# A third of the early v loads moved from GpSimd's casting DMA queue to SyncE's queue, with the cast done by GpSimd

## The chip, the cores and the metric

The kernel runs on one core of a Trainium2 chip. The metric is the device time of one execution in microseconds (us); lower is better. The engines are named as in the profile: PE (TensorE, with PEld for its weight loads), ACT (ScalarE), DVE (VectorE), POOL (GpSimd) and SP (SyncE). "q0" is the DMA queue that POOL issues into, "q1" the one of SP.

## The reference

Attention with a relative position bias for 8 batches of 8 heads, 576 positions and head size 64, followed by a feed-forward layer on the 4608 tokens:

```python
scores = scale * np.matmul(q, k.transpose(0, 1, 3, 2))      # q, k, v: (8, 8, 576, 64) float32
scores = scores + bias.transpose(2, 0, 1)[None, :, :, :]    # by bucketed distance, per head
attn = softmax(scores)
x = np.matmul(attn, v)            # to (4608, 512)
h = x @ w_in                      # (512, 2048)
g = np.maximum(0.01 * h, h)
out = g @ w_out                   # (2048, 512) -> (4608, 512) float32
```

## The kernel before

Work goes by pairs of heads: `items` lists the 32 pairs (b, p), four to a batch, and n counts them. For pair n, `qk_mm` makes score tiles on PE, `exp` turns them into bf16 on ACT, `band` multiplies the part near the diagonal by the bias factors `hk` on DVE, `av_tails` and `av` multiply by v on PE one pair later, and DVE divides by the row sums (`rcp`, `opair`). `x_transposes` turns the result into `xT`. When a batch is finished its tokens are ready for the feed-forward part, in token tiles T of 512: `ffn_in` (line 420) and `leaky` fill a buffer `gt` (pool `gt`, two buffers of 16 KB a partition), and `ffn_out` (line 447) reads it. The pieces of the feed-forward part are put between the attention steps from pair 4 on (`moe`), and what is left runs at the end (`moe_rest`). All orders are written out by hand: each engine runs its instructions in the order in which the program issues them.

v is kept in bf16 in two buffers `vn[b % 2]`, laid out [128 positions, 4 chunks c of positions, 8 heads, 65], where column 65 holds ones; the last 64 positions are in `v4`. DRAM holds float32, so every load of q, k, v and the weights goes through POOL's DMA queue, which casts on the way. The calls that matter, in POOL's order before the change:

- ahead of the loop: q and k of batch 0 and single heads 0 to 3 of v (`load_v_head`, line 125), `load_qk(1, 0, 4)`, then heads 4 to 7 of batch 0's v in four pieces (`load_v_part`, line 119), then `load_qk(1, 4, 8)` (line 112);
- at n = 0 (`loads`, called by `begin`): the first half of `w_in` (line 235), batch 1's v in four pieces, its tail (line 132), the second half of `w_in`, the first half of `w_out` (line 239);
- at n = 2: q and k of batch 2's lower heads, the second half of `w_out`;
- from n = 5 on, for batch b + 1 while batch b runs: at p = 1, 2 and 3 a one-element copy `tick` (line 621) waits until pair n - 2 is done, and then the loads of the next batch are issued, those of v at p = 1 and p = 2.

SP's queue holds at the start the small loads of the bias factors (`load_hk`, `load_hk4`, lines 192 and 199, the last of them `load_hk(4, H)`), and later the DMA transposes of q, k (line 265) and of the attention's result (line 387) and the stores of the output (line 466).

Of the kernel before, what the change touches and what calls it, by code (L numbers as in the profile page):

```python
# [10 lines left out]
FP32 = mybir.dt.float32  # L11
BF16 = mybir.dt.bfloat16
# [25 lines left out]
def kernel(  # L38
# [10 lines left out]
    nc = tc.nc  # L49

    B, H, S, D = q.shape
# [4 lines left out]
    P = 128  # L56
    n_pairs = H // 2
    NJ = S // P
# [3 lines left out]
    TT = 512  # L62
    n_tt = NT // TT
    n_fc = DF // P
# [11 lines left out]
    gt_pool = ctx.enter_context(tc.tile_pool(name="gt", bufs=2))  # L76
# [17 lines left out]
    NBUF = 2  # L94
# [4 lines left out]
    vn = [per.tile([P, NJ, H, D + 1], BF16, name=f"vn{i}") for i in range(NBUF)]  # L99
# [9 lines left out]
    def load_qk(b, h0, h1):  # L109
        i = b % NBUF  # L110
        for src, dst in ((q, qn[i]), (k, kn[i])):
            nc.gpsimd.dma_start(  # L112
                out=dst[0:RQ, h0:h1, :, :].rearrange("r h c d -> r h (c d)"),
                in_=src[b, h0:h1, :, :].rearrange("h (r c) d -> r h (c d)", c=NC),
            )

    def load_v_part(b, chunks, h0=0, h1=H):
        for c in chunks:
            nc.gpsimd.dma_start(  # L119
                out=vn[b % NBUF][:, c, h0:h1, 0:D],  # L120
                in_=v[b, h0:h1, c * P : (c + 1) * P, :].rearrange("h s d -> s h d"),
            )

    def load_v_head(b, h):
# [2 lines left out]
            in_=v[b, h, 0 : NJ * P, :].rearrange("(c s) d -> s c d", s=P),  # L127
        )

    def load_v_tail(b):  # L130
        for e in range(2):
            nc.gpsimd.dma_start(
                out=v4[b % NBUF][e * SL : (e + 1) * SL, :, 0:D],
                in_=v[b, e::2, NJ * P : S, :].rearrange("h s d -> s h d"),
            )

    def clear_v(eng, i):
        eng.memset(v4[i][:, :, D : D + 1], 1.0)
        eng.memset(vn[i][:, :, :, D : D + 1], 1.0)
# [39 lines left out]
    for j, (u, lo, w, m) in enumerate(groups):  # L179
        copy = nc.scalar.copy if j % 3 == 2 else nc.vector.tensor_copy  # L180
        copy(out=ub[:, C0 + lo : C0 + lo + m * w].rearrange("h (m w) -> h m w", w=w),
             in_=e8[:, u : u + m].unsqueeze(2).to_broadcast([H, m, w]))
    row = ub[:, :]
    nc.vector.tensor_copy(
        out=ub[:, C0 - BAND + 1 : C0],
        in_=bass.AP(tensor=row.tensor, offset=row.offset + C0 + BAND - 1,
                    ap=[list(row.ap[0]), [-1, BAND - 1]]),
# [3 lines left out]
    def load_hk(h0, h1):  # L191
        nc.sync.dma_start(
            out=hk[:, h0:h1, :],
            in_=bass.AP(tensor=udr, offset=h0 * UW, ap=[[1, P], [UW, h1 - h0], [1, BW]]),
        )

    def load_hk4(p0, p1):
        for e in range(2):
            nc.sync.dma_start(
                out=hk4[e * SL : (e + 1) * SL, p0:p1, :],  # L200
                in_=bass.AP(tensor=udr, offset=(2 * p0 + e) * UW + SL + P,
                            ap=[[1, SL], [2 * UW, p1 - p0], [1, P + SL]]),
            )
# [3 lines left out]
    load_hk(2, 4)  # L207
    load_hk4(1, n_pairs)
    load_hk(4, H)

    def mirrored(t, lo, hi):

        w = t.shape[-1]
        v = t[..., w - hi : w - lo]
        ap = [list(d) for d in v.ap]
        ap[-1][0] = -1
        return bass.AP(tensor=v.tensor, offset=v.offset + hi - lo - 1, ap=ap)
# [4 lines left out]
    load_v_head(0, 0)  # L222
    load_v_head(0, 1)
    load_v_tail(0)
    load_qk(0, 6, H)
    load_v_head(0, 2)
    load_v_head(0, 3)
    load_qk(1, 0, H // 2)
    load_v_part(0, range(NJ), 4, H)
    clear_v(nc.gpsimd, 1)  # L230
    load_qk(1, H // 2, H)

    def load_w_in(half):
        o = slice(half * (DF // 2), (half + 1) * (DF // 2))
        nc.gpsimd.dma_start(out=w_in_sb[:, :, o], in_=moe_w_in[:, o].rearrange("(c p) f -> p c f", p=P))

    def load_w_out(half):
        n = n_fc // 2
        nc.gpsimd.dma_start(
            out=w_out_sb[:, half * n : (half + 1) * n, :],  # L240
            in_=moe_w_out[half * n * P : (half + 1) * n * P, :].rearrange("(f p) e -> p f e", p=P),
        )
# [3 lines left out]
    qts, kts, ops_ = {}, {}, {}  # L246
# [151 lines left out]
    gts = {}  # L398
    rest = {"on": False, "turn": 0}

    def bank(name):

        if rest["on"]:
            turn = rest["turn"] = (rest["turn"] + 1) % 6
            if turn % 3 == 0:
                return ps_o_pool.tile([P, 512], FP32, name=name, tag=f"o{turn // 3}")
            if turn % 3 == 1:
                return ps_s_pool.tile([P, 512], FP32, name=name, tag="ps_s")
        return ps_m_pool.tile([P, 512], FP32, name=name, tag="m")

    def ffn_in(T, f, spare=None):
        if f == 0:
            gts[T] = gt_pool.tile([P, n_fc, TT], BF16, name="gt")
        t0 = T * TT
        if spare is None:
            pm = bank("pm1")
        else:
            pm = ps_o_pool.tile([P, 512], FP32, name="pm1", tag=f"o{spare}")
        for c in range(n_cc):
            nc.tensor.matmul(pm, lhsT=w_in_sb[:, c, f * P : (f + 1) * P], rhs=xT[c][:, t0 : t0 + TT],  # L420
                             start=(c == 0), stop=(c == n_cc - 1))
        return pm
# [61 lines left out]
    def step(kind):  # L484
        T, s = made[kind], at_piece[kind]
        at_piece[kind] = (s + 1) % n_fc
        if at_piece[kind] == 0:
            made[kind] += 1
        return T, s
# [5 lines left out]
    def piece_in(spare=None):  # L495
        T, s = step("in")
        leaky(T, s, ffn_in(T, s, spare))
# [51 lines left out]
    def moe_block():  # L549

        done = 0
        while not can("out") and can("in") and done < 4 and room["left"] > 0:
            T, f = step("in")
            leaky(T, f, ffn_in(T, f, 0 if done == 3 and room["left"] > 1 else None), done == 1)
            room["left"] -= 1
            done += 1
            if done < 3:
                yield
        while done < 2:
            done += 1  # L560
            yield
        if room["split"]:
            yield
            piece_out()
            piece_out()
        elif can("out") and room["left"] >= 4:
            for part in range(4):
                piece_out()
                room["left"] -= 1
                if part == 1:  # L570
                    yield
            moe(2, 0 if room["left"] > 1 else None)
        else:
            yield
            moe(2)
        yield
# [28 lines left out]
    tick = per.tile([1, 1], BF16, name="tick")  # L605

    def loads(n):

        b, p = items[n]
        if n == 0:  # L610
            load_w_in(0)
            load_v_part(1, range(NJ))
            load_v_tail(1)
            load_w_in(1)
            load_w_out(0)
        elif n == 2:
            load_qk(2, 0, H // 2)
            load_w_out(1)
        if b < 1 or p < 1 or b > B - 2:
            return  # L620
        nc.gpsimd.tensor_copy(out=tick, in_=ops_[n - 2][0:1, 0, 0:1])  # L621
        if p == 1:
            load_qk(b + 1, H // 2, H)
            load_v_part(b + 1, (0,))
        elif p == 2:
            load_v_part(b + 1, (1, 2, 3))
        else:
            load_v_tail(b + 1)
            if b + 2 < B:
                load_qk(b + 2, 0, H // 2)  # L630

    def begin(n):
        loads(n)
        if by_dma(n + 1):
            turn_ahead(n)
# [53 lines left out]
    n = n_pairs  # L689
# [24 lines left out]
    for n in range(n_pairs + 1, N + 1):  # L714
# [41 lines left out]
        if room["only"]:  # L756
            exp(n, 3, ps_b)
            moe(2)
            exp(n, 4, ps_c)
            score(n, 5)  # L760
            T, f = step("in")
            room["left"] -= 1

            def last_bands():
                band(n, 5)
                band(n, 4)

            leaky(T, f, ffn_in(T, f), True, last_bands)
            moe(room["left"])
            continue  # L770
# [44 lines left out]
```

## Time and profile before

| | us |
|---|---|
| median of 3 runs (lowest, highest) | 378.06 (377.69, 379.08) |
| profiled execution, its own time | 378.04 |
| span in the profile | 376.3 |
| PE busy | 366.1 (97%) |
| ACT busy | 239.9 (64%) |
| DVE busy | 199.1 (53%) |
| POOL busy | 77.3 (21%) |

The span is the time from the first to the last instruction; what the profiled execution took beyond it, 1.7 us, lies around it. TensorE's granted clock is 1.0 throughout. Times in the profile are counted from the start of the span. A row of a timeline gives start, duration, engine, line, operation, output and input tile, the count, and in brackets the idle time ahead of it with what ended it. A row of a DMA issue gives output and input, the queue, the count, the size and the time from issue to landing.

### The profile page before, as it was taken

What the parts mean: (1) busy time and instruction counts of PE and PEld (TensorE: products, weight loads), DVE (VectorE), ACT (ScalarE), POOL (GpSimd) and SP (SyncE); (2) the same over time, 40 slices, a digit from 0 to 9 for tenths busy, and PEclk for the clock granted to TensorE, in tenths of its full rate; (3) what the DMA queues carried; (4) which work ended last, traced back from release to release, by engine and by line L of the source; (5) the groups of instructions that cost most, each with busy time, mean ns of one, the idle gap of its engine ahead of it and who ended that gap; (6) DMA issues with size and microseconds to landing.
All of it is one profiled execution on the core that took longest, in us unless ns stands there. A gap on an engine that the chain in (4) does not pass through costs nothing.

```text
span 376.3 us, 8737 instructions
## 1 busy us (share of the span) xinstructions
PE 366.1 (97%) x3604; PEld 186.7 (50%) x3604; DVE 199.1 (53%) x502; ACT 239.9 (64%) x376; POOL 77.3 (21%) x118
## 2 busy tenths in 40 slices
PE   7879999999999999999999999999999999999996
PEld 3455555554555555555545545555555544444442
DVE  3678577777657666666755666655553300200221
ACT  5998886568856787777866666767777255055000
POOL 8763422333023303330323033100000000000000
PEclk9999999999999999999999999999999999999999
DMA  8999999998599959997998399453111000110212
GB/s 104 189 194 186 206 199 120 181 179 121 77 119 157 145 85 123 151 152 91 142 118 132 72 124 127 74 79 77 47 47 47 28 30 0 59 54 0 82 60 84
DMA packets 104351, 40.06 MB, mean 106 GB/s; under 512 B 83184, under 2 KB 98808, under 8 KB 104312
## 3 DMA queue, kind: packets, MB, share of 16 engines
q0 software_dynamic: 53696, 18.36, 47.2%
q1 hardware_dynamic: 50472, 21.02, 31.7%
q8 instruction: 28, 0.46, 0.5%
q10 hardware_dynamic: 144, 0.13, 0.1%
q14 instruction: 11, 0.09, 0.1%
HBM read 37.68 MB, written 9.45 MB: 125 GB/s over the span
## 4 chain that ended last, share of the span: by engine, by line
PE 89%; DMA 5%; POOL 2%; DVE 2%; ACT 1%; issue 1%; DVEq 0%; ACTq 0%; POOLq 0%
PE pm L447 34%; PE pm L420 32%; PE ps_o L372 10%; PE ps_s L312 8%; DMA vn<-in_v_dram 3%; PE ps_s L315 2%; DMA v<-in_v_dram 1%; PE ps_o L361 1%; PE ps_q L305 1%; DVE opair L376 1%; PE ps_tx L394 1%; PE ps_t L275 1%; ACT at L325 1%; POOL kn L112 1%; POOL qn L112 0%
## 5 line engine op out<-in xcount | busy, mean ns | idle before, releaser
L420 PE MATMUL pm<-xT,w_in_sb 128*128 128x512 bf16 x576 | 138.4, 379 | 0.1
L433 ACT ACTIVATE gt<-pm 128x512 bf16<-128x512 f32 x138 | 82.5, 603 | 86.2 <-PE pm L420 85.7
L447 PE MATMUL pm<-w_out_sb,gt 128*128 128x512 bf16 x576 | 132.5, 379 | 0.0
L325 ACT ACTIVATE at<-ps_s 128x1024 bf16<-128x1024 f32 x128 | 124.2, 1028 | 8.2 <-PE ps_s L312 8.1
L348 DVE TENSOR_TENSOR at<-at,hk 128x768 bf16<-128x768 bf16 (+3 forms) x160 | 71.0, 453 | 32.7 <-ACT at L328 19.9
L447 PEld LDWEIGHTS <-gt 128*128 128x128 bf16 x576 | 53.0, 98 | 60.6
L420 PEld LDWEIGHTS <-w_in_sb 128*128 128x128 bf16 x576 | 52.0, 98 | 54.8 <-issue 0.7
L465 DVE COPY y<-pm 128x512 f32<-128x512 f32 x33 | 22.8, 691 | 76.6 <-PE pm L447 76.6
L372 PE MATMUL ps_o<-vn,at 128*128 128x65 bf16 x1280 | 49.8, 194 | 0.4 <-DMA vn<-in_v_dram 0.4
L372 PEld LDWEIGHTS <-at 128*128 128x128 bf16 x1280 | 44.7, 97 | 9.5 <-issue 1.2
L312 PE MATMUL ps_s<-qt,kt 64*128 64x512 bf16 x256 | 40.1, 381 | 3.5 <-ACT at L325 3.0
L375 DVE RECIPROCAL rcp<-ps_o 128x5 f32<-128x5 f32 x64 | 12.3, 192 | 45.1 <-PE ps_o L372 45.1
L376 DVE TENSOR_TENSOR opair<-ps_o,rcp 128x320 bf16<-128x320 f32 x64 | 31.5, 492 | 3.3
L119 POOL DMA_DIRECT2D vn<-in_v_dram x32 | 29.6, 931 | 10.0 <-PE ps_s L312 5.6
L621 POOL COPY tick<-opair 1x1 bf16<-1x1 bf16 x18 | 4.7, 263 | 130.8 <-DVE opair L376 130.8
L312 PEld LDWEIGHTS <-kt 64*128 64x128 bf16 x256 | 8.4, 94 | 29.0 <-issue 21.5
L332 ACT ACTIVATE at<-ps_s 128x576 bf16<-128x576 f32 x32 | 21.8, 681 | 0.2 <-PE ps_s L316 0.2
L328 ACT ACTIVATE at<-ps_q 128x256 bf16<-128x256 f32 x64 | 21.5, 402 | 0.3 <-PE ps_q L305 0.2
L457 ACT COPY y<-pm 128x256 f32<-128x256 f32 x1 | 0.4, 372 | 27.5 <-DVE y L457 27.5
L294 DVE COPY kt<-tu 128x576 bf16<-128x576 bf16 x23 | 15.5, 674 | 0.0
L290 DVE COPY qt<-tu 128x576 bf16<-128x576 bf16 x23 | 15.0, 650 | 0.4 <-DMA tu<-pr 0.4
L112 POOL DMA_DIRECT2D qn<-in_q_dram x18 | 14.1, 782 | 4.2 <-PE ps_t L275 1.3
(57 smaller groups left out, 175.0 us busy)
## 6 DMA issues: line engine op xcount, KB each, us to landing
out_dram<-y SPq DMA_DIRECT2D x35, 256.0 KB, 2.3
qn<-in_q_dram POOLq DMA_DIRECT2D x14, 288.0 KB, 5.9
kn<-in_k_dram POOLq DMA_DIRECT2D x14, 288.0 KB, 7.1
vn<-in_v_dram POOLq DMA_DIRECT2D x28, 128.0 KB, 5.2
w_in_sb<-in_moe_w_in_dram POOLq DMA_DIRECT2D x2, 1024.0 KB, 12.9
w_out_sb<-in_moe_w_out_dram POOLq DMA_DIRECT2D x2, 1024.0 KB, 15.9
qn<-in_q_dram POOLq DMA_DIRECT2D x4, 144.0 KB, 4.3
kn<-in_k_dram POOLq DMA_DIRECT2D x4, 144.0 KB, 4.6
```

The costliest lines, as they stand in the source:

```text
L119: nc.gpsimd.dma_start(out=vn[b % NBUF][:, c, h0:h1, 0:D], in_=v[b, h0:h1, c * P : (c + 1) * P, :].rearrange("h s d -> s h d"),)
L312: nc.tensor.matmul(ps[:, e, :], lhsT=kt[r, u * P : (u + 1) * P], rhs=qt[r, 0:512], start=True, stop=True)
L325: nc.scalar.activation(at[:, :, u, 0:512], ps, AF.Exp, scale=scale)
L328: nc.scalar.activation(at[:, e, :, 512:S], ps[e][:, 0 : NJ * SL].rearrange("p (c i) -> p c i", i=SL), AF.Exp, scale=scale)
L332: nc.scalar.activation(at4[:, 0:S], ps.rearrange("p e i -> p (e i)")[:, 0:S], AF.Exp, scale=scale)
L348: nc.vector.tensor_tensor(out=o, in0=o, in1=m, op=ALU.mult)
L372: nc.tensor.matmul(ps[:, ic, :], lhsT=at[:, o : o + P], rhs=vn[b % NBUF][:, c, 2 * p + e, :], start=False, stop=(ic == NJ and c == NJ - 1))
L376: nc.vector.tensor_tensor(out=opair[:, :, e * D : (e + 1) * D], in0=ps[:, :, 0:D], in1=rcp.to_broadcast([P, NJ + 1, D]), op=ALU.mult)
L420: nc.tensor.matmul(pm, lhsT=w_in_sb[:, c, f * P : (f + 1) * P], rhs=xT[c][:, t0 : t0 + TT], start=(c == 0), stop=(c == n_cc - 1))
L433: nc.scalar.activation(g, pm, AF.Prelu, bias=0.0, scale=1.0, alpha=0.01)
L447: nc.tensor.matmul(pm, lhsT=gt[:, f, ts * P : (ts + 1) * P], rhs=w_out_sb[:, f, :], start=(f == 0), stop=(f == n_fc - 1))
L465: nc.vector.tensor_copy(out=y, in_=pm)
```

## The change

The four pieces of batch 0's upper heads, batch 1's v and batch 2's v are no longer loaded by POOL's casting queue. SP's queue copies them as float32 into a buffer `stage` that takes one of the two buffers of pool `gt` (tag "gt"), and POOL casts them from there into `vn` with `tensor_copy`, one instruction for each chunk.

- Batch 0's upper heads: `stage_v` stands behind `load_hk(4, H)` in SP's order; `cast_v` stands behind `load_qk(1, 4, 8)` in POOL's, ahead of the first half of `w_in`.
- Batch 1: at n = 3 a one-element copy on DVE into `stage`, reading pair 1's result, stands ahead of the four transfers; the casts follow in POOL's order, and behind them the first half of `w_out`, the lower q and k of batch 2 and the second half of `w_out`, which stood at n = 0 and n = 2.
- Batch 2: the one-element copies on POOL at n = 5 and n = 6 write into `stage` and stand ahead of two transfers each; the casts come at n = 7. Batches 3 to 7 are loaded as before.

```diff
+    stage = gt_pool.tile([P, 2 * NJ, H, D], FP32, name="stage", tag="gt")
+
+    def stage_v(b, chunks, h0=0, h1=H):
+        for c in chunks:
+            nc.sync.dma_start(
+                out=stage[:, c, h0:h1, :],
+                in_=v[b, h0:h1, c * P : (c + 1) * P, :].rearrange("h s d -> s h d"),
+            )
+
+    def cast_v(b, h0=0, h1=H):
+        for c in range(NJ):
+            nc.gpsimd.tensor_copy(out=vn[b % NBUF][:, c, h0:h1, 0:D], in_=stage[:, c, h0:h1, :])
...
     load_hk(4, H)
+    stage_v(0, range(NJ), 4, H)
...
     load_qk(1, 0, H // 2)
-    load_v_part(0, range(NJ), 4, H)
     clear_v(nc.gpsimd, 1)
     load_qk(1, H // 2, H)
+    cast_v(0, 4, H)
...
-            gts[T] = gt_pool.tile([P, n_fc, TT], BF16, name="gt")
+            gts[T] = gt_pool.tile([P, n_fc, TT], BF16, name="gt", tag="gt")
...
         if n == 0:
             load_w_in(0)
-            load_v_part(1, range(NJ))
             load_v_tail(1)
             load_w_in(1)
+        elif n == 3:
+            nc.vector.tensor_copy(out=stage[0:1, 0, 0, 0:1], in_=ops_[n - 2][0:1, 0, 0:1])
+            stage_v(1, range(NJ))
+            cast_v(1)
             load_w_out(0)
-        elif n == 2:
             load_qk(2, 0, H // 2)
             load_w_out(1)
         if b < 1 or p < 1 or b > B - 2:
             return
-        nc.gpsimd.tensor_copy(out=tick, in_=ops_[n - 2][0:1, 0, 0:1])
+        done = ops_[n - 2][0:1, 0, 0:1]
+        if b == 1 and p < 3:
+            nc.gpsimd.tensor_copy(out=stage[0:1, 2 * p - 2, 0, 0:1], in_=done)
+            stage_v(b + 1, (2 * p - 2, 2 * p - 1))
+        else:
+            nc.gpsimd.tensor_copy(out=tick, in_=done)
         if p == 1:
             load_qk(b + 1, H // 2, H)
+        if p == 1 and b > 1:
             load_v_part(b + 1, (0,))
-        elif p == 2:
+        elif p == 2 and b > 1:
             load_v_part(b + 1, (1, 2, 3))
-        else:
+        elif p == 3:
+            if b == 1:
+                cast_v(b + 1)
             load_v_tail(b + 1)
```

## The prediction

> **What bounds the kernel now.** I read the page's head and its chain first, then busy time by stage, then the timelines of the stage in which PE has gaps.
>
> ```profile
> span 376.3 us, 8737 instructions
> ...
> PE 89%; DMA 5%; POOL 2%; DVE 2%; ACT 1%; issue 1%; DVEq 0%; ACTq 0%; POOLq 0%
> PE pm L447 34%; PE pm L420 32%; PE ps_o L372 10%; PE ps_s L312 8%; DMA vn<-in_v_dram 3%; PE ps_s L315 2%; DMA v<-in_v_dram 1%; PE ps_o L361 1%; PE ps_q L305 1%; DVE opair L376 1%; PE ps_tx L394 1%; PE ps_t L275 1%; ACT at L325 1%; POOL kn L112 1%; POOL qn L112 0%
> ```
>
> The chain is PE's for 89%; the transfers on it are those of `v`, 4% together. Busy time by stage (length, then PE, PEld, DVE, ACT, POOL) shows where PE is not full:
>
> ```profile
> 17.00:23.00 6.00, 4.72 (x104) 3.22 (x99) 5.06 (x15) 5.52 (x8) 2.10 (x3) 1.00 1.58 199
> 23.00:29.00 6.00, 4.74 (x98) 3.18 (x97) 4.40 (x13) 5.52 (x8) 4.76 (x6) 1.00 1.28 201
> 29.00:35.00 6.00, 5.66 (x98) 3.53 (x95) 4.84 (x13) 5.72 (x10) 1.58 (x2) 1.00 1.99 176
> ...
> 120.00:298.00 178.00, 178.00 (x1843) 91.47 (x1842) 108.22 (x270) 127.28 (x201) 28.88 (x42) 1.00 0.75 99
> ```
>
> From 120 to 298 us PE has no gap at all, and there nothing that a load does can help. Before 35 us PE is idle for 1.28, 1.26 and 0.34 us of three stages; ACT is nearly full there (5.52 of 6), and the DMA share (the number before the GB/s) is above 1, that is, more than one packet in flight on each engine all the time. The start is the one place where the change can be felt, as a shift of everything behind it. PE's timeline there:
>
> ```profile
> 26.21 0.32 PE L372 MATMUL ps_o<-vn,at 128*128 128x65 bf16 x3
> 26.96 0.67 PE L372 MATMUL ps_o<-vn,at 128*128 128x65 bf16 x17 [0.43 <-DMA vn<-in_v_dram]
> ...
> 34.67 1.02 PE L420 MATMUL pm<-xT,w_in_sb 128*128 128x512 bf16 x4
> ...
> 39.75 0.78 PE L372 MATMUL ps_o<-vn,at 128*128 128x65 bf16 x20
> ...
> 61.89 1.89 PE L447 MATMUL pm<-w_out_sb,gt 128*128 128x512 bf16 x8
> ```
>
> Four needs are read here: batch 0's upper heads of `v` at 26.53 (they come 0.43 us late), the first half of `w_in` at 34.67, batch 1's `v` at 39.75, `w_out` at 61.89. What serves them is POOL's queue, here with the start of each issue:
>
> ```profile
> 11.88 0.70 POOL L112 DMA_DIRECT2D kn<-in_k_dram  x1
> 12.55 0.79 POOL L119 DMA_DIRECT2D vn<-in_v_dram  x1
> 13.65 1.50 POOL L119 DMA_DIRECT2D vn<-in_v_dram  x2 [0.32 <-DMA v<-in_v_dram]
> 15.37 0.74 POOL L119 DMA_DIRECT2D vn<-in_v_dram  x1 [0.22 <-issue]
> ...
> 19.43 0.67 POOL L112 DMA_DIRECT2D kn<-in_k_dram  x1 [1.28 <-DMA vn<-in_v_dram]
> 21.82 0.75 POOL L235 DMA_DIRECT2D w_in_sb<-in_moe_w_in_dram  x1 [1.72 <-DMA qn<-in_q_dram]
> 23.91 3.55 POOL L119 DMA_DIRECT2D vn<-in_v_dram  x4 [1.34 <-DMA kn<-in_k_dram]
> ```
>
> and the time from issue to landing, of the issues at 11.88, 15.37, 19.43 and 21.82, and of the last two of the four from 23.91:
>
> ```profile
> kn<-in_k_dram POOLq DMA_DIRECT2D x1, 288.0 KB, 11.5
> vn<-in_v_dram POOLq DMA_DIRECT2D x1, 64.0 KB, 11.5
> kn<-in_k_dram POOLq DMA_DIRECT2D x1, 288.0 KB, 9.5
> w_in_sb<-in_moe_w_in_dram POOLq DMA_DIRECT2D x1, 1024.0 KB, 12.1
> vn<-in_v_dram POOLq DMA_DIRECT2D x2, 128.0 KB, 11.9
> ```
>
> Start plus landing time gives an order of arrival: kn of batch 1's lower heads 23.4, v of batch 0's upper heads 26.9, kn of batch 1's upper heads 28.9, first half of `w_in` 33.9, v of batch 1 38.4 (last issue 26.6). The queue is served first in, first out without a pause, so the differences are service times: 3.5 us for v0 (my name for the four pieces), 2.0 for q and k between, 5.0 for `w_in`'s half, 4.5 for v1. Against the needs there is 0.8 us of slack for `w_in` and 1.3 for v1. The order is as tight as the work allows, and it is this order that the change breaks up.
>
> **The change, part by part.** (a) v0 leaves POOL's queue for SP's, behind `load_hk(4, H)`:
>
> ```profile
> 11.78 0.67 SPq L192 DMA_DIRECT2D hk<-u_row  x1
> 60.29 2.13 SPq L265 DMA_TRANSPOSE tu<-pr  x1
> ```
>
> SP does nothing between these two, so twelve more issues wait for nobody: v0's four, at 0.67 each, are out by 15.1. But their data stands behind hk in SP's queue. Packets of the two queues (q0 is POOL's, q1 SP's) in the microsecond from 17, and of SP's in that from 20:
>
> ```profile
> q0 software_dynamic: 157, 0.10, 68.7%
> q1 hardware_dynamic: 154, 0.12, 47.1%
> ```
> ```profile
> q1 hardware_dynamic: 13, 0.01, 3.3%
> ```
>
> So hk holds SP's queue until about 20 to 21, and while both queues have work they share the engines packet for packet. From 21 POOL's queue still has 2.4 us (to 23.4) and 2.0 us (q and k of batch 1's upper heads) to serve; SP's has v0, 3.5 us if a plain copy costs what the casting one does. Shared evenly, v0 ends at 21 + 7.0 = 28.0; at the latest with all that work, 28.9; if plain rows cost half, or SP's queue is served first, 24.5. I take 27.2, near the even share because the packet counts show one, a little below it because a copy without cast is hardly dearer.
>
> (b) Four casts of 128x256 on POOL. The trace has none; the nearest rows:
>
> ```profile
> L621 POOL COPY tick<-opair 1x1 bf16<-1x1 bf16 x18 | 4.7, 263 | 130.8 <-DVE opair L376 130.8
> masks.py:199 POOL TENSOR_SCALAR_AFFINE_SELECT ident<-ident 128x128 bf16<-128x128 bf16 x1 | 0.3, 287 | 0.1
> ```
>
> A cast costs between 0.26 (one element, nearly all of it start) and 0.57 us (twice the 128-wide one); I take 0.4 for 256 columns, and 0.8 for v1's and v2's 512, between 0.26 and 1.15. Only the last piece's cast counts, the others run while pieces arrive. v0 is ready at 27.6, and PE, which now waits from 26.53 to 26.96, waits 0.64 longer (ends: 0.43 less, if v0 lands by 24.5; 2.5 more, from 28.9 + 0.57). The Trainium skill, "GPSIMD Engine Reference", section 3.1, gives a body bound by its ports 1.03 cycles an element at 1.2 GHz: an estimate of 0.22 us for 256 columns without the start; by it v0 would be ready up to 0.2 us earlier. No run here shows it yet.
>
> (c) The casts stand in POOL's order before `load_w_in(0)`. That is the costly edit: an issue that left at 21.82 now waits for SP's transfer and the casts, to 27.6. What it then takes on an emptied queue is bounded by a load that finds no other of its queue:
>
> ```profile
> 105.35 0.82 POOL L112 DMA_DIRECT2D qn<-in_q_dram  x1
> ```
> ```profile
> qn<-in_q_dram POOLq DMA_DIRECT2D x1, 288.0 KB, 4.4
> ```
>
> 4.4 us, of which some 1.0 is service (half of the 2.0 above), so 3.4 of latency. `w_in`'s half lands at 27.6 + 3.4 + 5.0 = 36.0, for a need at 34.67: 1.3 late. Beside it runs v1 on SP's queue: free to go from 27.2, it has some 2.8 us for itself before `w_in`'s data starts to move (about 30.0, 2.4 after the issue), and the 1.7 us that are left push `w_in` to 37.7 if shared evenly: 3.0 late. Ends of this term: nothing (24.5 + 0.4 + 8.4 = 33.3, in time), and 4.9 (29.5 + 8.4 + 1.7 = 39.6). I take 2.0, midway between 1.3 and 3.0, because the plain copies' price decides and is not in the trace. The 0.64 of (b) lies inside it, since both hold the same queue of PE one after the other. Batch 1's lower k now shares its last 2.4 us with v0 too, and may come at up to 25.8; its wait also falls inside.
>
> (d) v1 leaves POOL's queue (3.55 us of POOL's issuing). Its gate is a one-element DVE copy at n = 3, before the last bands of pair 2:
>
> ```profile
> 24.21 1.12 DVE L348 TENSOR_TENSOR at<-at,hk 128x768 bf16<-128x768 bf16 x3
> ```
>
> It reads `opair` of pair 1, long done by then, and head 0 of a buffer whose casts read heads 4 to 7, so it should wait for nothing: 0.1 to 0.3 us, covered by ACT. SP's issues do wait for the casts; behind them in SP's order is nothing until 60.29. v1 is there at 33.4 and the last cast done by 35, before 39.75 plus the shift: nothing, with 5 us of cover; without it, rival 2.
>
> (e) `load_w_out` and batch 2's lower q and k come behind v1's casts on POOL, about a microsecond later than now, with over 20 us until 61.89. v2 goes by SP with casts at n = 7; it takes service time out of POOL's queue and its first reader is pair 8. The second `gt` buffer is asked for only by token tile 1, after batch 1 is finished, later than the last cast: nothing.
>
> The sum: +2.0 us, all from (c), on the profiled execution's 378.04 (376.3 of span and 1.7 around it); on the median of 378.06 that is 380.1.
>
> **The rivals.** 1, not slower: SP's copies are cheap or served early. v0 lands by 24.5, the cast is over at 24.9, PE's 0.43 us goes, and `w_in` at 33.3 is still in time: 377.6, no more, since ACT is full behind it. It decides if v0 is cast by 26. For it: the even share is only of packets, of another size. Against: it needs v0's 3.5 us halved. The Trainium skill, "DMA: Bandwidth & Descriptors", section "Specifications", has pieces under 512 B pay a read-modify-write; the writes of v in the casting load are 128 B, those into the new buffer a row of 1 or 2 KB, and by that rule this rival would come true. The packet counts of before cannot show it. Chance 0.24.
>
> 2, far slower: SP's queue gives way and v1 arrives last. `w_in`'s halves (5.0 each) and v1 (4.5) all finish together, from 30.0 at 44.5; without a cast that is 4.8 late for 39.75: 382.9. For it: a `w_in` packet carries far more bytes than one of v, so packet-for-packet sharing favours it. Against: v1's head start. 0.13.
>
> 3, a clash of GpSimd and VectorE: the casts fall among the bands at 24 to 31 us (0.37 each, from the row above), and if one of the two engines has to stand still for the other, two or three bands wait out a cast of 0.4 to 0.8: 1 to 2 us in a stretch where DVE leads PE closely, so +1 to +3: 379 to 381. The Trainium skill, "SBUF — State Buffer", section "Who interferes with whom", states just this lock, for a VectorE instruction with two SBUF inputs against a GpSimd one that reads SBUF. No row of before has the two together. 0.10.
>
> 4, the gate does not do what it says: if the one-element copy waits for all casts of the shared buffer, DVE stands until 27.6, 3 us past its turn, with two bands of 0.37 and the copy of the next k behind it; I put half of the 3 us, 1.5, on top of my 2.0: 381.6. 0.05.
>
> **How the numbers follow.** My case has 0.45; its spread of 1.1 to 3.0 lies on both sides of 0.5% (1.9 us, about what a measurement of this kernel can tell from no change), 0.27 above and 0.18 below. Slower by more: 0.27 + 0.13 + 0.05 + half of rival 3 = 0.50. Within: 0.18 + 0.24 + 0.05 = 0.47. Faster by over 0.5% would need two thirds of all of PE's 2.9 us of idle time from 17 to 35, of which transfers hold 0.43: 0.03. The range reaches from rival 1's 377.5 to rival 2's 383.2.
>
> **What would show it.** In the profile after: the first L420 of PE has a wait on `w_in_sb` of 1 to 3 us in front of it; the `w_in` issue stands at 26 to 29 us on POOL, behind four casts of 0.3 to 0.6 us; the L372 at 26 us waits on POOL's cast; from 45 us on PE is as full as before. Wrong: if `w_in` is issued before 25, if L420 does not wait, or if PE's largest new wait is on `vn` near 40 us (rival 2) or on bands (rivals 3 and 4).

## The result and the profile after

The changed kernel takes 383.29 us (median of 4 runs, 382.24 to 385.51) against 377.88 (377.51 to 379.08) for the kernel before on the same chip: ratio 1.0148, interval 1.0110 to 1.0186. Slower, as forecast, but by 5.4 us and not by 2.0, and 0.1 us beyond the range.

The page of the profiled execution (its own time 382.24), head and chain:

```profile
span 380.5 us, 8703 instructions
...
PE 85%; DMA 7%; SPq 2%; ACT 1%; DVE 1%; issue 1%; another core or an unknown queue 1%; POOL 0%; DVEq 0%
PE pm L461 32%; PE pm L434 31%; PE ps_o L386 10%; PE ps_s L326 7%; DMA stage<-in_v_dram 3%; DMA w_in_sb<-in_moe_w_in_dram 3%; PE ps_s L329 1%; SPq L134 1%; PE ps_o L375 1%; PE ps_q L319 1%; DMA u_row<-ub 1%; SPq L212 1%; PE ps_t L289 1%; DMA tabT<-in_bias_table_dram 1%
```

PE's share of the chain fell from 89 to 85%, and two transfers stand on it with 3% each: `stage` (v0) and `w_in`. The chain in order of time (start, duration, what) shows them one behind the other:

```profile
13.54 3.72 SPq L134
17.26 0.04 issue
17.31 10.64 DMA stage<-in_v_dram
27.95 0.05 issue
28.00 0.24 POOL vn L141
28.24 0.11 issue
28.35 10.07 DMA w_in_sb<-in_moe_w_in_dram
38.42 0.05 issue
38.46 0.39 PE pm L434
```

v0's last piece lands at 27.95, its cast ends near 28.4, `w_in`'s first half leaves at 28.35 in place of 21.82, and it lands at 38.42 in place of 33.9. The timeline of PE (new line numbers: 386 was 372, 434 was 420, 461 was 447):

```profile
27.20 0.19 PE L386 MATMUL ps_o<-vn,at 128*128 128x65 bf16 x1 [1.13 <-POOL vn L141]
27.54 0.19 PE L386 MATMUL ps_o<-vn,at 128*128 128x65 bf16 x1 [0.16 <-POOL vn L141]
28.46 1.10 PE L386 MATMUL ps_o<-vn,at 128*128 128x65 bf16 x17 [0.73 <-POOL vn L141]
...
38.46 1.04 PE L434 MATMUL pm<-xT,w_in_sb 128*128 128x512 bf16 x3 [0.55 <-DMA w_in_sb<-in_moe_w_in_dram]
...
43.56 0.78 PE L386 MATMUL ps_o<-vn,at 128*128 128x65 bf16 x20
...
65.82 1.89 PE L461 MATMUL pm<-w_out_sb,gt 128*128 128x512 bf16 x7
```

Against before: the 17 products of pair 2 start 1.50 later, the first feed-forward matmul 3.79, the fifth pair's products 3.81, the first `w_out` matmul 3.93. From there to the end the distance is the same; the rest of the span's 4.2 us lies behind the last store. So nearly all of it arises before 38.5 us, where it was looked for. The median lies another 1.05 us above this execution. The 1.10 in the third row stands against 0.67 before for the same 17 matmuls. Two windows say why (length, PE, PEld, DVE, ACT, POOL, then the granted clock):

```profile
25.80:28.50 2.70, 0.68 (x14) 0.34 (x7) 0.31 (x2) 1.37 (x2) 1.25 (x4) 0.87 0.67 146
28.50:34.50 6.00, 6.00 (x80) 4.23 (x79) 3.71 (x10) 3.29 (x6) 4.65 (x7) 0.50 1.14 211
```

PE stood nearly idle from 26.1 to 28.5, and the granted clock was 0.50 for the six microseconds that followed. The Trainium skill, "TensorE: Matmul & The Clock Gate", Part 1, has the clock at half after an idle window of about 3.4 us; here 2.4 us with two short matmuls in between were enough. The prediction had no such term, so the experiments had to say whether it sets the time.

### The profile page after: what moved, and what is told of

Its sections match the earlier page's. It is cut to its first block, busy times and chain, and to the rows that moved or that the text cites. A ratio compares the mean times of both kernels' runs of the same rounds, so it can differ in the third digit from the quotient of the medians.

```text
span 380.5 us, 8703 instructions
## 1 busy us (share of the span) xinstructions
PE 364.7 (96%) x3549; PEld 188.2 (49%) x3604; DVE 200.5 (53%) x503; ACT 240.2 (63%) x376; POOL 72.6 (19%) x118
## 4 chain that ended last, share of the span: by engine, by line
PE 85%; DMA 7%; SPq 2%; ACT 1%; DVE 1%; issue 1%; another core or an unknown queue 1%; POOL 0%; DVEq 0%
PE pm L461 32%; PE pm L434 31%; PE ps_o L386 10%; PE ps_s L326 7%; DMA stage<-in_v_dram 3%; DMA w_in_sb<-in_moe_w_in_dram 3%; PE ps_s L329 1%; SPq L134 1%; PE ps_o L375 1%; PE ps_q L319 1%; DMA u_row<-ub 1%; SPq L212 1%; PE ps_t L289 1%; DMA tabT<-in_bias_table_dram 1%
## 5 line engine op out<-in xcount | busy, mean ns | idle before, releaser
L434 PE MATMUL pm<-xT,w_in_sb 128*128 128x512 bf16 x543 | 136.2, 379 | 2.4 <-DMA w_in_sb<-in_moe_w_in_dram 0.6
L461 PE MATMUL pm<-w_out_sb,gt 128*128 128x512 bf16 x555 | 130.8, 379 | 1.1
L362 DVE TENSOR_TENSOR at<-at,hk 128x768 bf16<-128x768 bf16 (+3 forms) x160 | 72.3, 460 | 33.4 <-ACT at L342 19.8
L434 PEld LDWEIGHTS <-w_in_sb 128*128 128x128 bf16 x576 | 51.9, 98 | 55.4 <-DMA w_in_sb<-in_moe_w_in_dram 0.9
L386 PE MATMUL ps_o<-vn,at 128*128 128x65 bf16 x1280 | 51.0, 195 | 2.0 <-POOL vn L141 2.0
L386 PEld LDWEIGHTS <-at 128*128 128x128 bf16 x1280 | 45.6, 98 | 11.6 <-issue 3.2
L390 DVE TENSOR_TENSOR opair<-ps_o,rcp 128x320 bf16<-128x320 f32 x64 | 31.5, 492 | 3.3
L119 POOL DMA_DIRECT2D vn<-in_v_dram x20 | 19.0, 956 | 2.9 <-PE ps_o L386 1.7
```

What stands on the lines that cost most here:

```text
L119: nc.gpsimd.dma_start(out=vn[b % NBUF][:, c, h0:h1, 0:D], in_=v[b, h0:h1, c * P : (c + 1) * P, :].rearrange("h s d -> s h d"),)
L362: nc.vector.tensor_tensor(out=o, in0=o, in1=m, op=ALU.mult)
L386: nc.tensor.matmul(ps[:, ic, :], lhsT=at[:, o : o + P], rhs=vn[b % NBUF][:, c, 2 * p + e, :], start=False, stop=(ic == NJ and c == NJ - 1))
L390: nc.vector.tensor_tensor(out=opair[:, :, e * D : (e + 1) * D], in0=ps[:, :, 0:D], in1=rcp.to_broadcast([P, NJ + 1, D]), op=ALU.mult)
L461: nc.tensor.matmul(pm, lhsT=gt[:, f, ts * P : (ts + 1) * P], rhs=w_out_sb[:, f, :], start=(f == 0), stop=(f == n_fc - 1))
```

## The experiments

Theories. A: the order of arrival; v0 comes late because the queues are served packet for packet, and `w_in` is issued behind its casts. B: the halved clock. C: staging and casting cost by themselves, wherever they stand. D: the queues share bytes or time evenly, or the plain copy is dear by its bytes. E: only the issue behind the casts costs, not the sharing. "Before" is the kernel before on the same chip: 378.24, 377.61 and 377.85 in the three groups.

**1. The change again** (no edit), since its runs lay 3 us apart.

> The changed kernel as it is, for a second profile, because its four runs lie between 382.24 and 385.51. Theory A (the order of arrival: v0 late, and the first half of w_in issued behind v0's casts and landing near 38.4 us): the same chain again, 382 to 385.5, and where a run is longer, batch 1's v is the late one (a PE wait on a cast near 43 to 45 us). Theory B (PE's gap of 2.4 us at 26 us halves the granted clock for 6 us, and that is what costs): the length follows how long the clock stays at half. Theory C (staging and casting cost wherever they stand, by clashes of GpSimd and VectorE): the bands on DVE are longer than in the kernel before.

384.14 us, ratio 1.0159 (1.0116 to 1.0202). Window 28 to 34 us, in the first profile and in this one:

```profile
28.00:34.00 6.00, 5.54 (x70) 3.98 (x71) 3.21 (x9) 2.79 (x5) 5.14 (x8) 0.50 1.09 203
```
```profile
28.00:34.00 6.00, 4.23 (x83) 2.83 (x83) 4.83 (x10) 5.08 (x8) 5.12 (x8) 1.00 1.12 215
```

PE's timeline in this one:

```profile
39.02 1.04 PE L434 MATMUL pm<-xT,w_in_sb 128*128 128x512 bf16 x4 [1.76 <-DMA w_in_sb<-in_moe_w_in_dram]
```

The clock stayed at 1.00, and still L434 started at 39.02: what PE saved it spent waiting for `w_in`. v0 had not come earlier (its last piece landed at 27.89, against 27.95). PE had come later: it reached these products at 27.55 and not at 25.86, since already the start of this execution of the same kernel had run behind that of the first:

```profile
28.39 0.67 PE L386 MATMUL ps_o<-vn,at 128*128 128x65 bf16 x17 [0.45 <-POOL vn L141]
```

It was not batch 1's v that made this run longer, as had been expected, but a second loss, 1.87 us, behind pair 8:

```profile
86.32 0.29 PE L319 MATMUL ps_q<-qt,kt 64*128 64x64 bf16 x7 [1.68 <-DVE opair L390]
```
```profile
84.73 0.90 DVE L304 COPY qt<-tu 128x576 bf16<-128x576 bf16 x1 [1.90 <-DMA tu<-pr]
```

DVE waits for the first of two DMA transposes on SP's queue. The row of the two, and the packets of both queues in the two microseconds from 84:

```profile
71.54 9.14 SPq L279 DMA_TRANSPOSE tu<-pr  x2
...
q0 software_dynamic: 491, 0.17, 89.9%
q1 hardware_dynamic: 494, 0.13, 89.7%
```

DVE goes on at 84.71, 13.2 us after that transpose was issued; the next one, issued at 81.95, took 12.7 us to land (the median of 23 was 4.0 before). At the end of the wait the transposes went packet for packet beside POOL's later loads. This second loss is in this profile and in that of run 3, and not in the first profile of the change or in that of run 4.

**2. Batches 1 and 2 staged, v0 back on POOL's queue.**

```diff
     load_hk(4, H)
-    stage_v(0, range(NJ), 4, H)
...
     load_qk(1, 0, H // 2)
+    load_v_part(0, range(NJ), 4, H)
...
-    cast_v(0, 4, H)
```

> Batch 0's upper heads back on POOL's casting queue; batches 1 and 2 staged as in the change. Theory A: w_in's first half is issued near 22 us again and lands by 34.5 to 35.5, no PE gap at 26 us beyond 0.43 us; what is left is batch 1's v, which shares packet for packet with w_in and may be 0 to 1.5 us late: 378 to 379.6. Theory B: the same, as there is no gap to halve the clock. Theory C: most of the loss stays, 381 or more, since eight of the twelve casts and transfers stay.

385.30 us, ratio 1.0172 (1.0136 to 1.0209): a miss for A as I had sized it, and by the time alone C had won. The profile says otherwise. Packets in the microseconds from 31 and from 35, PE's largest wait, and the last cast on POOL:

```profile
q0 software_dynamic: 190, 0.14, 90.1%
q1 hardware_dynamic: 192, 0.05, 36.4%
```
```profile
q0 software_dynamic: 93, 0.19, 100.0%
q1 hardware_dynamic: 93, 0.02, 17.4%
```
```profile
PE ps_o L385 <- POOL vn L141: 3.5, 3, 1.9
```
```profile
43.46 0.62 POOL L141 CAST vn<-stage 128x512 bf16<-128x512 f32 x1 [0.35 <-DMA stage<-in_v_dram]
```

`w_in` is in time here (it landed at 33.71), but beside its packets of 2 KB SP's queue gets one packet of 256 B for each: 0.02 MB in a microsecond against 0.19. Batch 1's v, 4096 packets, is cast at 44.1 for a need at 39.7. This is rival 2 of the prediction, in a kernel where v1 had no gap in POOL's transfers to slip through. The wait is not the whole loss. Behind it the granted clock stood near half, and here PE had nothing else to wait for:

```profile
44.00:50.00 6.00, 5.87 (x76) 3.98 (x76) 2.85 (x7) 0.69 (x2) 4.79 (x9) 0.53 0.78 98
```

PE is 4.3 us behind the kernel before when the last cast is done, and 6.45 at 50.41. So some 2.2 us of this run's loss are B's.

**3. Only v0 staged.**

> Only batch 0's upper heads staged and cast; batches 1 and 2 as before the change. Theory A: v0 is cast at 28.4 again, w_in is issued there and lands near 36.8 without batch 1's v beside it; PE's own lateness with the half clock (about 37.9 at the first feed-forward matmul) then sets the end: 380.5 to 382. Theory B: 382 or more, the same loss as the whole change. Theory C: a third of the loss, 379.5.

382.31 us, ratio 1.0107 (1.0080 to 1.0134). `w_in` left at 28.72, and L434 waited for it:

```profile
37.35 1.04 PE L434 MATMUL pm<-xT,w_in_sb 128*128 128x512 bf16 x4 [0.84 <-DMA w_in_sb<-in_moe_w_in_dram]
```

That is as in A, but with the clock at 1.00, so it was not PE's own lateness that set it. The time, 0.3 us above A's range, lies in B's, and B is not the reason. Without v1 beside it `w_in` landed 8.59 us after its issue. The profile loses 1.4 us more at pairs 7 to 9, where DVE waits 2.46 and 0.56 us for transposes; batches 1 and 2 are loaded here as before the change, so that loss does not come from their staging. C's third of the loss is ruled out.

**4. PE kept busy while it waits.**

```diff
             av_tails(n - 1)
+            if n == 3:
+                hold(9)
             av(n - 1, 0)
```

`hold(9)` makes nine matmuls on the zeroed tile `junk`.

> The changed kernel with nine matmuls on a zeroed tile (128x512, about 0.22 us each, not read by anybody) on PE between the tails of pair 2 and its products with v, so that PE is busy while it waits for v0. Theory A: the granted clock stays at 1.0, but w_in lands at 38.4 all the same and the first feed-forward matmul waits 2 us for it: no gain, within 0.5 us of the changed kernel. Theory B: a gain of 1.5 to 2 us. Theory C: no gain.

383.49 us, ratio 1.0152 (1.0107 to 1.0196): no gain. From 24.5 us on the clock stayed at 1.00, v0's last cast ended at 30.3 in this run, and L434 waited for `w_in` as before:

```profile
40.03 1.04 PE L434 MATMUL pm<-xT,w_in_sb 128*128 128x512 bf16 x4 [0.82 <-DMA w_in_sb<-in_moe_w_in_dram]
```

B falls for the change: its halved clock lay in the shadow of `w_in`. This execution had a stretch of half clock too, earlier, ahead of the added matmuls:

```profile
20.50:24.50 4.00, 3.45 (x52) 2.57 (x51) 2.10 (x6) 3.10 (x4) 0.18 (x1) 0.57 1.27 198
```

**5. The same bytes in a quarter of the packets.** v's positions are staged as rows of four neighbours, piece by piece of one head (batch 0) or two, and cast by heads. The scores keep their order of positions; the kernels of runs 5, 9 and 10 leave out what would match the two, and serve for their times alone.

```diff
+    def stage_w(b, heads):
+        for h0, h1 in heads:
+            nc.sync.dma_start(
+                out=wide[:, h0:h1, :],
+                in_=v[b, h0:h1, 0 : NJ * P, :].rearrange("h (s c) d -> s h (c d)", c=NJ),
+            )
...
-    stage_v(0, range(NJ), 4, H)
+    stage_w(0, ONES)
```

> The changed kernel with the same bytes staged in rows four times as long: four neighbouring positions of v go to one partition (1 KB a row in place of 256 B), so SP's queue has a quarter of the packets; casts are of the same size, by heads. It leaves v's positions in another order than the reference. Theory A, in the form that the queues are served packet for packet (in the run with batches 1 and 2 staged the counts per us were 217 and 218, 190 and 192, 93 and 93): v0 lands near 23, w_in is issued by 25 and lands by 34.5, batch 1's v is there before 36; no wait but small ones: 378 to 379.5. Theory D (the queues share time or bytes evenly, or the plain copy is dear by its bytes): the same bytes arrive as late as before, 382 to 385.

380.45 us, ratio 1.0077 (1.0047 to 1.0108): half of the loss is gone with not one byte less, so D falls; A's range, which ended at 379.5, was missed too. v0's last piece is cast from 25.32 and `w_in` leaves at 26.22, later than I had expected, and PE still waits for it:

```profile
25.32 0.96 POOL L156 CAST vn<-stage 128x256 bf16<-128x256 f32 x1 [0.58 <-DMA stage<-in_v_dram]
26.22 0.76 POOL L269 DMA_DIRECT2D w_in_sb<-in_moe_w_in_dram  x1
```
```profile
36.73 1.04 PE L454 MATMUL pm<-xT,w_in_sb 128*128 128x512 bf16 x4 [1.63 <-DMA w_in_sb<-in_moe_w_in_dram]
```

Alone, the wide rows move no more bytes than the short ones. In the microsecond from 27 this run's SP queue has the engines to itself:

```profile
q1 hardware_dynamic: 290, 0.28, 101.3%
```

0.28 MB is also what the change's 256 B rows moved alone (the row with 1120 packets below). So what the wide rows save had been lost in the sharing, and not through a price of each short row by itself. Pair 2's two heads are also complete sooner here, since the pieces go by head; but `w_in` stands behind all four casts, so its earlier start does not come from that.

**6. `w_in` issued ahead of the casts** (256 B rows).

```diff
-    cast_v(0, 4, H)
...
             load_w_in(0)
+            cast_v(0, 4, H)
             load_v_tail(1)
```

> The changed kernel with the first half of w_in issued on POOL ahead of v0's casts, not behind them. Theory A, packet for packet: w_in lands in time, but its 2 KB packets now hold up v0's 256 B ones one for one; v0 lands at 30 to 32 and PE waits 4 to 6 us at 26 us: 382 to 385, no better than the change. Theory E (only the issue behind the casts costs, the sharing does not): v0 at 28, w_in at 34: 379 to 380.5.

386.88 us, ratio 1.0243 (1.0222 to 1.0263): the obvious repair makes it worse, 9.3 us above the kernel before where the change was 5.4 and 5.9 above, and 1.9 above A's range. From 27 us, and v0's last cast:

```profile
q0 software_dynamic: 92, 0.19, 97.9%
q1 hardware_dynamic: 91, 0.02, 18.6%
```
```profile
33.71 0.40 POOL L141 CAST vn<-stage 128x256 bf16<-128x256 f32 x1 [0.59 <-DMA stage<-in_v_dram]
```

Now v0 goes one for one with `w_in` and comes at 34. E falls; A had it at 30 to 32. Behind PE's waits for the casts (4.6 us) the clock stood at 0.50 from 33 to 38 us, with `w_in` landed at 33.2, so here too a part of the loss is the clock's.

**7. v0 cut by head, `w_in` between the casts.**

```diff
-    cast_v(0, 4, H)
+    cast_head(4)
+    cast_head(5)
...
             load_w_in(0)
+            cast_head(6)
+            cast_head(7)
```

> The changed kernel with v0's four pieces cut by head and not by chunk, and with w_in's first half issued on POOL behind the casts of heads 4 and 5 and ahead of those of heads 6 and 7. Theory A: heads 4 and 5 are half of the packets, cast near 26.4; w_in is issued 2 us earlier than in the change and lands near 36.5: 380.5 to 382.5, a gain of 1.5 to 2 us on the change. Theory E: the same. Theory C (staging costs as such): no gain.

387.15 us, ratio 1.0243 (1.0212 to 1.0274): a miss. Pair 2's heads were there in time and `w_in` left at 26.75, but batch 1's v then started beside it and not ahead of it (first issue at 28.65, against 24.71 in the change, since each of its pieces overwrites rows of all four heads in `stage` and waits for the last cast), and its last cast began at 46.46; PE waited 3.7 us on the casts. In the change itself three of v1's four pieces landed by 31.5, in the gap that POOL's queue left while it waited for v0. One of the two big transfers is late in either order.

**8. The kernel before with v0 by head** (no staging): `load_v_head(0, h)` for heads 4 to 7 in place of `load_v_part(0, ...)`.

> The kernel before the change, with batch 0's upper heads loaded by POOL's casting queue in four pieces by head in place of four by chunk (the same packets in another order), so that the two heads that pair 2 needs are complete after half of them. Theory A: they land near 25.4 and PE's wait of 0.43 us at 26.5 goes, nothing else moves: 0.3 to 0.5 us faster, 377.5 to 378. If PE's wait is not what sets the end there: no change.

377.71 us, ratio 1.0002 (0.9985 to 1.0019). PE's wait on `vn` is gone from the profile, and the pairs run 0.25 us earlier from the third on; the times do not tell it from no change. So even the whole wait that the change could remove is not measurable. No version tried beats the kernel before.

**9. Wide rows and `w_in` first together** (edits 5 and 6).

> Both suspected costs taken away together: the bytes staged in rows of 1 KB (a quarter of SP's packets; v's positions then stand in another order than the reference), and the first half of w_in issued on POOL ahead of v0's casts. Theory A, packet for packet and nothing else: v0 lands near 24 as with the wide rows alone, w_in by 34.5, batch 1's v before 36, and the whole loss is gone: 377.5 to 378.8. Theory E (the issue behind the casts is what costs, not the sharing): the same here, but with 256 B rows w_in first should have gained, and it lost. Theory C (staging and casting cost as such): 380 or more stays.

378.76 us, ratio 1.0023 (1.0008 to 1.0038). No wait on any transfer of v or `w_in` is left, with all twelve pieces staged and all twelve casts in place:

```profile
34.73 1.02 PE L453 MATMUL pm<-xT,w_in_sb 128*128 128x512 bf16 x4
```

0.9 us of the change's 5.4 to 5.9 are left, so over four fifths of the loss are accounted for by the two causes together; C is left with at most 0.4%.

**10. Batches 1 and 2 staged in wide rows.**

> Batch 0's upper heads back on POOL's queue; batches 1 and 2 staged in rows of 1 KB (v's positions of these two in another order than the reference). With 256 B rows the same kernel took 385.3, since batch 1's v, 4096 packets, went one for one with w_in's and came at 43.4. Theory A: 1024 packets in 256 KB pieces pass beside w_in's half in time; v lands before 37 and PE's wait on its casts goes: 377.8 to 379.3. Theory D (bytes or time shared evenly): no gain, 384 to 386.

378.78 us, ratio 1.0023 (1.0004 to 1.0043), where the 256 B rows took 385.3. The profiled execution, at 380.79 the longest of ten, shows PE waiting 1.75 for `w_in` beside v1's larger packets.

**11. Only batch 2 staged.**

> Only batch 2's v staged in its 256 B rows and cast; batches 0 and 1 and the order of the weights as before the change. Its first reader is pair 8, near 66 us, and nothing of the start is touched. Theory A: no loss from the start; at most a part of a microsecond from later transposes of q and k that find the queues fuller: 377.8 to 378.8. Theory C: a third of the loss, 379.5 to 380.5.

378.55 us, ratio 1.0019 (0.9997 to 1.0040): not told from no change.

## Why the prediction was wrong, and what in it was right

The side, the place and the mechanism were right: a shift that arises before 40 us, through `w_in` issued behind v0's casts. The term that failed is (c), 2.0 us taken, 3.8 measured (3.79 at L434); its ends were 0 and 4.9. Of the signs that I had named, the `w_in` issue behind four casts and the wait of L372 on a cast came; the wait in front of the first feed-forward matmul was 0.55, below the 1 to 3 that I gave, since the halved clock had made PE itself late.

- The landing of v0: taken at 27.2, measured 27.95. I read the counts 157 and 154 as an even share of time, and then went below it because a plain copy might be cheaper. What is equal is the counts, as the pairs above and these, from the change's window 20 to 21, say:

```profile
q0 software_dynamic: 197, 0.14, 90.9%
q1 hardware_dynamic: 195, 0.05, 37.2%
```

  Whoever has the smaller packets loses: v's 256 B against the 1.5 KB of q and k or the 4 KB of `w_in` at their source. The Trainium skill, "DMA: Bandwidth & Descriptors", section "Queues, rings and completion order", has each engine take its queues in turn, packet by packet, with typically 9 to 17 descriptors to a packet. The trace agrees in that the counts are equal (197 and 195); how many of the profile's packets make one turn, such counts do not show.
- The flight of `w_in`: 8.4 us alone, 9.1 taken, 10.07 measured, the upper end that I had worked out and then halved. Alone it took 8.59 in run 3. Its rate beside v1 (first two rows, change, from 33 us) and alone (the row behind them, before, from 27):

```profile
q0 software_dynamic: 83, 0.17, 93.4%
q1 hardware_dynamic: 71, 0.02, 13.7%
```
```profile
q0 software_dynamic: 115, 0.21, 114.1%
```

  Without the two choices the even shares that I had worked out give 28.0 + 0.4 + 8.4 + 1.7 = 38.5, and 38.46 came. That they fit so well is in part luck: v1, which they have through 3.4 us after `w_in`'s data starts to move, had its last piece there at 39.0 (see (d)).

  Both choices leaned the same way, towards cheap plain copies. They are not cheap: alone, SP's queue moved 1120 packets of v in a microsecond of the change, POOL's casting one 1218 in the run with only batch 2 staged.

```profile
q1 hardware_dynamic: 1120, 0.28, 125.8%
```
```profile
q0 software_dynamic: 1218, 0.15, 254.4%
```

  So rival 1 found no support: the casting load moves no fewer packets in a microsecond, though its packets stay twice as long on the engines (254.4% for 1218 against 125.8% for 1120). The read-modify-write rule that I cited for it from the Trainium skill ("DMA: Bandwidth & Descriptors", Specifications) is not tested by that: the plain copies went in packets of 256 B, and not in the rows of 1 or 2 KB that I had counted on, so both kinds lie under its 512 B; run 5's rows of 1 KB lie above it and moved the same 0.28 MB alone.
- The casts: 0.40 us for 256 columns, as taken; 0.62 for 512 at the least, under the 0.8 taken. The estimate of 0.22 us for 256 columns without the start, worked out from the Trainium skill, "GPSIMD Engine Reference", section 3.1, agrees with the difference between the two.
- (b), v0's own wait: 0.64 more was forecast, 1.50 came. That it would halve the clock I did not see; runs 1 and 4 show that in the change this cost nothing beside `w_in`.
- (d), v1 ready by 35 with 5 us of cover: wrong. Its last cast ended at 39.8, and at 42.4 in the second profile, and only PE's own lateness kept that out of the chain. Rival 2, held at 0.13 for the change, is what run 2 shows: the wait of 3.5 us on the casts, with the halved clock behind it.
- (e), nothing from the later loads: a loss came there that I had not counted. The transposes of pairs 9 and 10 can come late, by 1.90 us in the second profile of the change and by 2.46 in run 3, where the later loads are those of before; so it is not shown that the moved loads are the reason. The same loss would be enough for the 1.05 us by which the median lies above the profiled execution, but only two executions of the change were profiled.
- Rival 3: the bands on DVE took 460 ns in the mean against 453, 1.3 us in all over 160 of them, so the lock between GpSimd and VectorE did not decide. Casts of 0.40 that took up to 0.96 (run 5), and of 0.62 up to 0.98, would fit it, with GpSimd as the one that waits; no run tests it. Rival 4: the gate on DVE took 0.13 us without a wait.

## What to carry to other kernels

Before a transfer is moved to an idle queue, compare the size of its rows with that of the packets on the queue that stays busy: here two queues that both had work were served packet for packet, so short rows crawled beside long ones, and a second queue was no second lane. An instruction that waits for another queue's transfer must not stand ahead of an issue that the critical path needs; but where the order in one queue was already tight, moving that issue up only makes the other transfer late. A fall of the granted clock is not yet a cause: look for what PE would have waited for without it. In the change that was `w_in`; in run 2 there was nothing, and the clock cost 2.2 us.

## What the runs showed of the hardware that I had not expected

Where two DMA queues both had much to move, they moved equal numbers of packets, from 93 and 93 in one microsecond (run 2) to 491 and 494 in two (run 1), whatever their sizes (128 B to 2 KB written); for the last packets of v1 it did not hold (83 and 71 in the change), and why is open. A gap of 2.4 us on PE, broken by two matmuls of 0.19, was followed by a granted clock of 0.50 for six microseconds; in run 4 the clock fell to half at 21 us with no gap above 0.85 us on PE in the five microseconds before. And a single issue on SP's queue took 3.72 us in the change where the one before it took 0.56; what held it up is not shown.
